# Ranks of a token tile in a PSUM bank of their own, and a new order of the steps behind the first half tiles

## The chip, the core and the metric

The kernel runs on one core of a Trainium2 chip. A core has a matrix engine (TensorE, in the rows PE, its weight loads PEld), VectorE (DVE), ScalarE (ACT), GpSimdE (POOL) and a queue that issues transfers (SyncE, SP); each runs its own list of instructions in the order in which the program was written, and semaphores hold an instruction until what it reads is there or what it overwrites has been read. Matrix products land in PSUM, in eight banks of 2 KB per partition. The metric is the time of one execution on the device in microseconds (us), as the median of several.

## The reference: what is computed

Three parts follow each other, on 4 x 768 = 3072 tokens with 8 heads of 48, so rows of 384:

```python
for t in range(S):                       # delta-rule attention, per batch and head
    y[:, :, t] = q_t @ state
    state = state + beta_t * outer(k_t, v_t - k_t @ state)
x = ((x @ w_a) * (x @ w_b)) @ w_out      # 384 -> 1536 -> 384
logits = x @ w_gate + modality_bias[modality_id]     # 8 experts
e = argmax(logits); gate = softmax(logits)[e]
out[token] = gate * (relu(x @ w1[e]) @ w2[e])        # 384 -> 1024 -> 384
```

All is float32; the kernel splits most operands into two float16 parts (hi and lo) and multiplies three of the four pairs.

## The kernel before

**Stages.** The attention is cut into 6 chunks of 128 steps by 4 batches, so 24 blocks `g` of 128 tokens. A block's steps have names by stage: `a_*` normalises the keys and makes their Gram matrix, `l_*` inverts a 32x32 triangle (a long chain of two VectorE operations per step, lines 621 and 626), `m1_mm` to `m4_mm` widen that inverse to 128, `p_*` makes the masked query-key product, and `s1_mm`, `s2_mm`, `s3_mm`, `s4_mm` carry the state. Two blocks make a token tile `t` of 256 rows for the second part: `f_mm(t, m)` is 18 matmuls for one of twelve 128-wide slices `m` of x @ w_a and x @ w_b (lines 334 to 336, PSUM tile `pab`); `f_a` copies one product (ACT, line 300, `a`), `f_ab` multiplies by the other (DVE, line 346), `f_hi` rounds to float16 (ACT, line 300, `g`), `f_lo` takes the rest (DVE or POOL, line 356, `g`), and `o_mm(t, m)` multiplies that slice by w_out and adds it into the two output tiles `po` (six matmuls, lines 367 to 369). The first token tile is worked as two half tiles, t = -2 and -1. `o_mm(t, 11)` completes a tile; then it is routed.

**Routing of a token tile.** `r_lg` (DVE, lines 388 to 394) makes logits, maximum, index and the one-hot tile `oh`; `r_mx` (lines 401 to 404) reduces both `po` tiles to their largest magnitude (`mo`); `r_hi` (ACT, line 410) and `r_lo` (DVE, line 416) read `po` again and write the rows. `r_rk` counts, with five matmuls of 8 columns on `oh` (lines 434 to 438), how many earlier tokens went to each expert, and `r_po` (DVE, lines 446 to 450) turns that into a slot number; `r_sc` scatters the row there. For the first ten tiles (`RQ = 10`) `r_rk` writes 24 columns behind the 392 columns of the tile's own `po` bank.

**The last part** gathers the rows per expert in slots `s` (`h_mm`, `g_mm`), with weights loaded and split on the way; it begins when the last token tile's products are done.

**What sets the order.** Every piece of work is a step declared with `do(...)`, which gives its engine, the steps it comes after and the buffers it takes. The table `ORDER` lists the 3613 steps by number; `emit` runs through it, and each engine executes its own steps in that sequence. `PICK` gives the engine of each step that could run on several. The PSUM pools bound what can be ahead: `ps_ab` has 2 banks for `pab`, `ps_o` two for `po`, `psg` two for the Gram, `m` and `p` steps, and `pss` two for the state steps (`pk`, `pu`, `py`, `pS`), all eight together. A step that takes a bank of a pool waits until the readers of the step that had it before are done.

Of the kernel before, what the change touches and what calls it, by code (L numbers as in the profile page):

```python
# [7 lines left out]
F32 = mybir.dt.float32  # L8
# [15 lines left out]
RQ = 10  # L24
# [167 lines left out]
def kernel(ctx, tc, k, q, v, beta, w_a, w_b, w_out, modality, w_gate, mbias, w1, w2, out):  # L192
    nc = tc.nc
    C, B, H, D = 6, 4, 8, 48
    NG = C * B
# [162 lines left out]
    def o_mm(t, m):  # L358
        g = GT[t, m]
        t, hs = (0, (t + 2,)) if t < 0 else (t, (0, 1))  # L360
        for h in hs:
            if m == 0:
                PO[2 * t + h] = ps_o.tile([128, WO + 3 * E], F32, name="po")
# [1276 lines left out]
```

## Time and profile before

| | |
|---|---|
| median of 3 runs | 959.95 us (955.12, 959.95, 961.57) |
| the profiled execution | 962.67 us, span 960.9 us |
| granted TensorE clock, mean | 0.949 |
| PE, PEld busy | 870.3 us (91%), 696.6 us (72%) |
| DVE, ACT, POOL busy | 722.1 us (75%), 542.6 us (56%), 299.9 us (31%) |

An engine's row of tenths shows its busy share in 40 slices of the span, PEclk the clock that was granted to TensorE in each. A row of waits says which engine's instruction sat idle for whose, the total, how often, and the longest. A matmul's row shows about 0.3 us for each, but the next one starts 0.11 to 0.17 us later, so that durations of neighbours overlap: what a group of matmuls costs is read from their starts.

### The profile page before, as it was taken

How to read it: one execution, taken by the hardware profiler on the slowest of the kernel's cores; microseconds unless marked ns; L12 is line 12 of the kernel's file. 1: busy time of each engine (PE TensorE's matmuls, PEld its weight loads, DVE VectorE, ACT ScalarE, POOL GpSimd, SP SyncE). 2: the span in 40 equal slices, each digit the busy share in tenths (PEclk: the TensorE clock that was granted, in tenths of full speed). 3: DMA queues.
4: the chain of work that ended last, by engine and by line, in shares of the span. 5: the costliest groups of instructions: out<-in, count | busy, mean ns of one | idle time of the engine just before them, and what ended most of it. 6: DMA issues, size and time to landing. Idle time of an engine off the chain costs nothing. (4 is left out here: it accounts for less than half of the span.)

```text
span 960.9 us, 30560 instructions
## 1 busy us (share of the span) xinstructions
PE 870.3 (91%) x11996; PEld 696.6 (72%) x11996; DVE 722.1 (75%) x1728; ACT 542.6 (56%) x1077; POOL 299.9 (31%) x442
## 2 busy tenths in 40 slices
PE   3446788799999999999999999999999999999996
PEld 1324577688777777888787888878878777878884
DVE  6899498776998799859995999454768885655551
ACT  3635676456754556656654655455466566555551
POOL 4421012433651344216331223023223342333331
PEclk9876659899999999999999999999999999999998
DMA  7896688684766546864667445432267899999980
GB/s 201 243 251 172 172 168 188 155 218 77 125 175 173 119 83 143 191 145 93 118 159 158 84 102 122 77 59 43 72 216 236 245 328 268 293 274 270 284 223 20
DMA packets 266066, 161.99 MB, mean 169 GB/s; under 512 B 188173, under 2 KB 245309, under 8 KB 265920
## 3 DMA queue, kind: packets, MB, share of 16 engines
q1 hardware_dynamic: 262288, 148.70, 64.0%
q0 software_dynamic: 3632, 11.29, 3.1%
q8 instruction: 99, 1.62, 0.7%
q14 instruction: 47, 0.39, 0.1%
HBM read 95.52 MB, written 30.31 MB: 131 GB/s over the span
## 5 line engine op out<-in xcount | busy, mean ns | idle before, releaser
L334 PE MATMUL pab<-xt,wa 128*128 128x256 f16 (+1 forms) x468 | 123.0, 267 | 1.9 <-DVE a L346 1.7
L335 PE MATMUL pab<-xt,wa 128*128 128x256 f16 (+1 forms) x468 | 122.7, 267 | 0.0
L336 PE MATMUL pab<-xt,wa 128*128 128x256 f16 (+1 forms) x468 | 122.7, 267 | 0.0
L334 PE MATMUL pab<-xt,wb 128*128 128x256 f16 (+1 forms) x468 | 122.4, 266 | 0.0
L335 PE MATMUL pab<-xt,wb 128*128 128x256 f16 (+1 forms) x468 | 122.4, 266 | 0.0
L336 PE MATMUL pab<-xt,wb 128*128 128x256 f16 (+1 forms) x468 | 122.4, 266 | 0.0
L303 DVE SCALAR_TENSOR_TENSOR w1l<-w1f,w1h 128x1024 f16<-128x1024 f32 x66 | 76.9, 1220 | 49.7 <-ACT w1h L300 39.4
L300 ACT ACTIVATE a<-pab 128x256 f32<-128x256 f32 (+1 forms) x156 | 56.6, 365 | 90.3 <-PE pab L336 66.9
L346 DVE SCALAR_TENSOR_TENSOR a<-pab,a 128x256 f32<-128x256 f32 (+1 forms) x156 | 61.9, 399 | 53.1 <-ACT a L300 52.0
L369 PE MATMUL po<-wo,g 128*128 128x392 f16 x288 | 95.8, 333 | 5.0 <-POOL g L356 2.4
L367 PE MATMUL po<-wo,g 128*128 128x392 f16 x288 | 95.7, 332 | 0.0
L368 PE MATMUL po<-wo,g 128*128 128x392 f16 x288 | 95.5, 332 | 0.0
L300 ACT ACTIVATE g<-a 128x256 f16<-128x256 f32 (+1 forms) x156 | 61.3, 397 | 45.5 <-DVE a L346 43.4
L1286 PE MATMUL pH<-xg_t,w1h 128*128 128x128 f16 x504 | 85.4, 219 | 0.0
L1287 PE MATMUL pH<-xg_t,w1h 128*128 128x128 f16 x504 | 85.4, 219 | 0.0
L1288 PE MATMUL pH<-xg_t,w1l 128*128 128x128 f16 x504 | 85.3, 219 | 0.0
L621 DVE TENSOR_TENSOR tmp<-A,T 128x31 f32<-128x31 f32 (+15 forms) x186 | 76.7, 412 | 2.1
L626 DVE TENSOR_TENSOR T<-T,tmp 128x31 f32<-128x31 f32 (+15 forms) x186 | 74.5, 400 | 2.0
L735 POOL TENSOR_TENSOR tl<-ttf,th 128x1024 f16<-128x1024 f32 x19 | 42.5, 2238 | 87.4 <-ACT th L300 57.8
L1315 PE MATMUL po<-w2h,hh 128*128 (+1 forms) x200 | 65.2, 326 | 2.1 <-ACT w1h L300 1.1
L300 ACT ACTIVATE w1h<-w1f 128x1024 f16<-128x1024 f32 x66 | 64.9, 1047 | 1.0 <-DMA w1f<-in_moe_w_dram 0.7
L1317 PE MATMUL po<-w2h,hl 128*128 (+1 forms) x200 | 65.2, 326 | 0.0
(315 smaller groups left out, 2825.1 us busy)
## 6 DMA issues: line engine op xcount, KB each, us to landing
w1f<-in_moe_w_dram SPq DMA_DIRECT2D x66, 512.0 KB
w2f<-in_moe_w_dram SPq DMA_DIRECT2D x32, 384.0 KB
gsc<-gs SPq DMA_DIRECT2D x22, 512.0 KB
bq<-aq SPq DMA_DIRECT2D x48, 128.0 KB
bk<-ak SPq DMA_DIRECT2D x40, 128.0 KB
qt<-in_q_dram SPq DMA_DIRECT2D x24, 192.0 KB
kt<-in_k_dram SPq DMA_DIRECT2D x24, 192.0 KB
raw<-in_moe_w_a_dram SPq DMA_DIRECT2D x12, 384.0 KB
```

The lines of the kernel that those rows point to most:

```text
L300: S_.activation(out=out, in_=in_, func=ACTF.Copy, scale=scale)
L303: V.scalar_tensor_tensor(out=out, in0=in_, scalar=scale, in1=hi, op0=ALU.mult, op1=ALU.subtract)
L334: T_.matmul(out=p[:, i], lhsT=wa[i][0][:, kk, sl], rhs=xt[:, kk], start=(kk == 0), stop=False)
L335: T_.matmul(out=p[:, i], lhsT=wa[i][0][:, kk, sl], rhs=xt[:, KD + kk], start=False, stop=False)
L336: T_.matmul(out=p[:, i], lhsT=wa[i][1][:, kk, sl], rhs=xt[:, kk], start=False, stop=(kk == KD - 1))
L367: T_.matmul(out=po, lhsT=g[:, 0, sl], rhs=wo[0][:, m], start=(m == 0), stop=False)
L368: T_.matmul(out=po, lhsT=g[:, 0, sl], rhs=wo[1][:, m], start=False, stop=False)
L369: T_.matmul(out=po, lhsT=g[:, 1, sl], rhs=wo[0][:, m], start=False, stop=(m == KF - 1))
L621: V.tensor_tensor(out=LN[c, 2], in0=A[:, j + 1 : 32, j : j + 1].to_broadcast([128, n, w]), in1=T[:, j : j + 1, 0:w].to_broadcast([128, n, ...
L1286: T_.matmul(out=pH[:, u], lhsT=wh[kk][:, sl], rhs=xt[:, kk], start=(kk == 0), stop=False)
L1287: T_.matmul(out=pH[:, u], lhsT=wh[kk][:, sl], rhs=xt[:, KD + kk], start=False, stop=False)
L1288: T_.matmul(out=pH[:, u], lhsT=wl[kk][:, sl], rhs=xt[:, kk], start=False, stop=(kk == KD - 1))
```

## The change

The rank counts get a tile of their own, `prk`, from the pool `pss` (its tag `ps`, which the state steps use too), for the first ten token tiles; `po` loses its 24 extra columns. So `po` no longer waits for `r_po` before it is given to the next token tile; `r_rk` takes one of the two `pss` banks until `r_po` has read it; `w_open`, which gives the attention's space to the last part, comes after `r_po(9)`. The numbers from the 1056th entry of `ORDER` on are new: of the steps, 302 of 669 on PE stand in another place in that engine's list (by 0.9 places in the mean over all, 7 at most), 643 of 1273 on DVE, 484 of 938 on ACT, 120 of 279 on POOL and 176 of 433 on SP. No step changes its engine, and none is added or removed.

```diff
-    2022, 1008, 1007, 989, 1982, 2026, 2023, 990, 1009, 2032, 2027, 947, 1010, 1985, 2028, 991, 2037, 2029, 992, 1031, 2033, 948, 1986, 1993, 993,
...
+    2441, 2442, 603, 1443, 1613, 2454, 2455, 1555, 1556, 2463, 1469, 646, 647, 648, 649, 2464, 2465, 2436, 2446, 1600, 2460, 2461, 1444, 2437, 2447,
...
@@ o_mm
-                PO[2 * t + h] = ps_o.tile([128, WO + 3 * E], F32, name="po")
+                PO[2 * t + h] = ps_o.tile([128, WO], F32, name="po")
@@ r_rk
-        pr = PO[2 * t][:, WO : WO + 3 * E] if t < RQ else M2["q"].tile([128, DM], F32, name="po2")[:, 0 : 3 * E]
-        R["pr"] = pr = pr.rearrange("p (i e) -> p i e", e=E)
+        if t < RQ:
+            R["pr"] = pr = pss.tile([128, 3, E], F32, name="prk", tag="ps")
+        else:
+            R["pr"] = pr = M2["q"].tile([128, DM], F32, name="po2")[:, 0 : 3 * E].rearrange("p (i e) -> p i e", e=E)
@@ the steps
-               take=[(f"ps_o{g % 2}", 1, [(r_hi, g), (r_lo, g), (r_lg, g // 2), (r_mx, g // 2), (r_po, g // 2)]) for g in ([t + 2] if half else [2 * t, 2 * t + 1])] if m == 0 else [])
+               take=[(f"ps_o{g % 2}", 1, [(r_hi, g), (r_lo, g), (r_lg, g // 2), (r_mx, g // 2)]) for g in ([t + 2] if half else [2 * t, 2 * t + 1])] if m == 0 else [])
-        do(r_rk, (t,), "PE", 0.1, o + 0.1, after=[(r_lg, t)] + ([(w_open,)] if t >= RQ else []), take=[("ps_q", 2, [(r_po, t)])] if t >= RQ else [])
+        do(r_rk, (t,), "PE", 0.27, o + 0.1, after=[(r_lg, t)] + ([(w_open,)] if t >= RQ else []), take=[("pss" if t < RQ else "ps_q", 2, [(r_po, t)])])
-    do(w_open, (), "-", 0.0, 0.0, after=[(c_end,)] + [(x_tr, g) for g in range(2, NG)] + [(p_lo, NG - 1, 1), (s3_lo, NG - 1), (l_o2, C - 1)])
+    do(w_open, (), "-", 0.0, 0.0, after=[(c_end,), (r_po, RQ - 1)] + [(x_tr, g) for g in range(2, NG)] + [(p_lo, NG - 1, 1), (s3_lo, NG - 1), (l_o2, C - 1)])
```

Lines behind 430 move down by two (the ranks' matmuls from 434 to 436, `r_po` from 446 to 448).

**The first place is on PE, the ranks of token tile 1.** The matmuls of `r_rk(1)` read the one-hot tile `oh` and write `po` before and `prk` now; `pab` is the up product of tile 2, `pk` is `s1_mm(8)`, `pg` the Gram step `a_mm(12)`. Before:

```order
L336 MATMUL pab_4403<-xt_3875,wb1_88 128x256
L434 LDWEIGHTS tri_92
L434 MATMUL po_3712<-oh_4394,tri_92 128x8
...
L438 MATMUL po_3712<-oh_4394,ones_93 128x8
L795 LDWEIGHTS ak_1634
L795 MATMUL pk_4450<-sst0_131,ak_1634 128x48
```

And now:

```order
L585 MATMUL pg_4507<-ak_4247,bk_4307 128x128
L436 LDWEIGHTS tri_92
L436 MATMUL prk_4531<-oh_4376,tri_92 128x8
...
L440 MATMUL prk_4531<-oh_4376,ones_93 128x8
L334 LDWEIGHTS wa0_85
L334 MATMUL pab_4555<-xt_3870,wa0_85 128x256
```

The ranks stood behind `f_mm(2,0)`; now `s3_mm(6)` and the two `a_mm` of block 12 stand between that and them, and two more `f_mm` and `s4_mm(6)` come before `s1_mm(8)`.

**The second place is on DVE, the same tile:** `lg` to `oh` is `r_lg`, `mo` and `io` are `r_mx`, and `pq` begins `r_po`, which frees the ranks' bank. Before:

```order
L394 TENSOR_TENSOR oh<-iota_95,ef 128x16
L401 TENSOR_REDUCE mo<-po 128x1 x2
...
L404 RECIPROCAL io<-mo 128x2
L303 SCALAR_TENSOR_TENSOR ul<-pu,uh 128x384
L346 SCALAR_TENSOR_TENSOR a<-pab,a 128x256
...
L416 SCALAR_TENSOR_TENSOR row<-po,io,row 128x384
...
L865 SCALAR_TENSOR_TENSOR xh<-py,iy,xh 128x384
...
L621 TENSOR_TENSOR tmp<-A,T 128x255
L446 TENSOR_TENSOR pq<-po,off 128x16
```

And now:

```order
L394 TENSOR_TENSOR oh<-iota_95,ef 128x16
L303 SCALAR_TENSOR_TENSOR ul<-pu,uh 128x384
L401 TENSOR_REDUCE mo<-po 128x1 x2
...
L404 RECIPROCAL io<-mo 128x2
L346 SCALAR_TENSOR_TENSOR a<-pab,a 128x256
L303 SCALAR_TENSOR_TENSOR wl<-w,wh 128x384
L319 TENSOR_REDUCE my<-py 128x1
...
L322 RECIPROCAL iy<-my 128x1
L448 TENSOR_TENSOR pq<-prk,off 128x16
```

`r_po(1)` stands behind five other steps where there were twenty.

**The third place is on PE, slices 5 to 10 of token tile 2.** Of each `f_mm` (`pab`) and `o_mm` (`po` with its slice `g`) one matmul is shown. Before:

```order
L334 MATMUL pab_5097<-xt_3875,wa0_85 128x256
...
L367 MATMUL po_4720<-wo0_89,g_4964 128x392
...
L367 MATMUL po_4720<-wo0_89,g_5093 128x392
...
L367 MATMUL po_4720<-wo0_89,g_5128 128x392
...
L367 MATMUL po_4720<-wo0_89,g_5154 128x392
...
L334 MATMUL pab_5182<-xt_3875,wa0_85 128x256
...
L334 MATMUL pab_5216<-xt_3875,wa0_85 128x256
```

And now:

```order
L334 MATMUL pab_5096<-xt_3870,wa0_85 128x256
...
L367 MATMUL po_4778<-wo0_89,g_4974 128x392
...
L367 MATMUL po_4778<-wo0_89,g_5074 128x392
...
L334 MATMUL pab_5149<-xt_3870,wa0_85 128x256
...
L334 MATMUL pab_5179<-xt_3870,wa0_85 128x256
...
L367 MATMUL po_4778<-wo0_89,g_5201 128x392
...
L367 MATMUL po_4778<-wo0_89,g_5207 128x392
```

Four `o_mm` stood in a row behind `f_mm(2,8)`, the last of them its own product; now `f_mm(2,9)` and `f_mm(2,10)` stand between the second and the third.

## Rows read from the trace of the kernel before

**Rows 1.** The page: span, TensorE's busy time, the granted clock in 40 slices.

```profile
span 960.9 us, 30560 instructions
PE 870.3 (91%) x11996; PEld 696.6 (72%) x11996; DVE 722.1 (75%) x1728; ACT 542.6 (56%) x1077; POOL 299.9 (31%) x442
...
PEclk9876659899999999999999999999999999999998
```

**Rows 2.** Busy time by stretch: PE, PEld, DVE, ACT, POOL, clock, DMA share, GB/s.

```profile
0.00:205.00 205.00, 136.36 (x1745) 103.32 (x1746) 165.89 (x406) 110.05 (x238) 60.65 (x108) 0.78 0.79 194
205.00:760.00 555.00, 543.53 (x8004) 442.35 (x8002) 438.56 (x1186) 325.22 (x697) 175.44 (x267) 1.00 0.57 132
...
240.00:600.00 360.00, 351.70 (x5445) 285.37 (x5443) 313.12 (x835) 215.39 (x460) 122.99 (x169) 1.00 0.61 132
```

**Rows 3.** Waits of PE and PEld, 200 to 770 us: total, times, longest.

```profile
PE po L434 <- DVE mo L401: 3.2, 4, 1.4
PE po L369 <- DVE g L356: 2.3, 5, 0.8
PE pab L334 <- DVE a L346: 1.7, 3, 0.8
PE py L848 <- DVE ul L303: 1.1, 2, 0.7
PE po L434 <- ACT row L410: 0.8, 1, 0.8
...
PEld L369 <- DVE g L356: 5.7, 9, 1.1
```

**Rows 4.** Order of time, the ranks of token tile 1.

```profile
269.35 0.17 DVE L394 TENSOR_TENSOR oh<-iota,ef 128x16 f16<-128x16 f32 x1
269.44 1.01 DVE L401 TENSOR_REDUCE mo<-po 128x1 f32<-128x384 f32 x2
...
270.05 0.17 PE L434 MATMUL po<-oh,tri 128*128 128x8 f16 x1 [1.35 <-DVE mo L401]
...
279.94 0.17 DVE L446 TENSOR_TENSOR pq<-po,off 128x16 f32<-128x16 f32 x1
...
280.62 0.17 DVE L450 CAST pi<-pf 128x2 int32<-128x2 f32 x1
```

**Rows 5.** Order of time, the ranks of token tile 3.

```profile
372.35 0.17 DVE L394 TENSOR_TENSOR oh<-iota,ef 128x16 f16<-128x16 f32 x1
...
373.04 0.17 PE L434 MATMUL po<-oh,tri 128*128 128x8 f16 x1 [0.65 <-DVE mo L401]
```

**Rows 6.** Order of time, the end of `o_mm(2, 8)` and the start of `f_mm(2, 9)`.

```profile
303.89 0.33 PE L368 MATMUL po<-wo,g 128*128 128x392 f16 x1
...
304.05 0.42 DVE L356 TENSOR_TENSOR g<-a,g 128x256 f16<-128x256 f32 x1
...
304.53 0.34 PE L369 MATMUL po<-wo,g 128*128 128x392 f16 x1 [0.31 <-DVE g L356]
...
304.70 0.33 PE L367 MATMUL po<-wo,g 128*128 128x392 f16 x1
...
305.20 0.27 PE L334 MATMUL pab<-xt,wa 128*128 128x256 f16 x1
...
305.31 0.27 PE L335 MATMUL pab<-xt,wa 128*128 128x256 f16 x1
```

**Rows 7.** Groups of instructions, 205 to 760 us: busy, mean ns, idle before.

```profile
L300 ACT ACTIVATE a<-pab 128x256 f32<-128x256 f32 (+1 forms) x134 | 50.6, 380 | 78.9 <-PE pab L336 61.5 <-DVE g L356 7.9 <-POOL g L356 5.8
L346 DVE SCALAR_TENSOR_TENSOR a<-pab,a 128x256 f32<-128x256 f32 (+1 forms) x134 | 55.6, 417 | 48.8 <-ACT a L300 48.2
L300 ACT ACTIVATE g<-a 128x256 f16<-128x256 f32 (+1 forms) x134 | 54.6, 412 | 41.6 <-DVE a L346 39.7 <-PE po L369 1.1 <-DVE sf L885 0.3
L356 DVE TENSOR_TENSOR g<-a,g 128x256 f16<-128x256 f32 x102 | 48.3, 478 | 14.8 <-ACT g L300 13.5 <-ACT ttf L300 1.0
```

**Rows 8.** Waits over the whole span, the costliest that a transfer ended.

```profile
PEld L765 <- DMA bq<-aq: 11.0, 2, 9.9
```

206 rows, old and new, of the table ORDER are left out of this document.

## The prediction, written before the result was known

> **What bounds the kernel now.** I read the page first. TensorE is busy for 91% of the span, and the clock that it was granted lies between 0.5 and 0.9 of full speed in the first eight slices of 24 us and in the top tenth from then on [rows 1]. Then the busy time by stretch: until 205 us TensorE works 136.36 of 205 us at a mean clock of 0.78; from 205 to 760 us it works 543.53 of 555 us at the full clock [rows 2]. On every engine the order is unchanged up to a place that lies between 225 and 231 us of this execution, and the slots behind 760 us keep nearly all of theirs. So what the new order can act on is the middle stretch, and there TensorE sets the pace: it sits idle for 555 - 543.53 = 11.5 us, 1.2% of the span. VectorE is close behind it, with 313.12 of 360 us between 240 and 600 us [rows 2], so a step that TensorE waits for is often not late in itself but stands in VectorE's line.
>
> Third, the waits say what those 11.5 us are [rows 3]: 3.2 + 0.8 = 4.0 us by the ranks' first matmul (five waits), 2.3 us by `o_mm` for the rest `g` that `f_lo` makes, 1.7 us by `f_mm` for a `pab` bank that `f_ab` still reads, and the other 3.5 us in small pieces, the largest 1.1 us by `s3_mm` for `ul`. The second is larger than it looks: the weight loads wait 5.7 us at nine places for the same `g`. A matmul of `o_mm` is shown for 0.33 us and the next starts 0.17 us later (304.53 and 304.70) [rows 6], so each such wait hides some 0.16 us under a row's end: 2.3 + 9 x 0.16 = 3.7 us.
>
> **The change, term by term.** Nothing is added: the five rank matmuls are the same five, with another target. All terms are of waits; a minus is a gain.
>
> *1. The ranks' wait.* In tile 1 `oh` is done at 269.35 + 0.17 = 269.52 us, but the first rank matmul starts at 270.05, right after the first of two reductions over `po` (269.44 + 0.55) [rows 4]. In tile 3 it is 372.52 and 373.04 [rows 5]. So 0.5 us of each wait are owed to a reader of the same `po` tile, and the rest is early arrival. With `prk` the first part goes. The second shrinks because ranks stand later: behind the tile's last `o_mm` there was TensorE work of 2.6, 2.4, 1.7, 2.3, 2.3 and 2.6 us in tiles 1, 2, 4, 5, 7 and 8, and now it is 4.5, 4.8, 5.2, 7.1, 5.8 and 3.9 us (steps between them in the two orders, at 18 x 0.11 = 2.0 us for an `f_mm` and 6 x 0.17 = 1.0 us for an `o_mm` by the starts in [rows 6], the others by their starts likewise). In tile 3 ranks keep their place and save 0.5 us. I take -3.6 of the 4.0 us. Bounds: -4.0 and 0.
>
> *2. `o_mm` waiting for `f_lo`.* From the end of `f_mm` four instructions follow one another, 0.38 + 0.42 + 0.41 + 0.48 = 1.7 us if no one is ahead of them [rows 7]. At the third place shown, `f_lo` ended at 304.47 and TensorE restarted at 304.53 [rows 6]. Of the 132 pairs of full tiles, 43 had less than 4.6 us of TensorE work between `f_mm` and its `o_mm`, and 12 have now; the median goes from 6.3 to 8.1 us. I scale the 3.7 us by 12/43 and get 1.0 left: -2.7. Bounds: -3.7, and 0 if VectorE's line is what is late.
>
> *3. `f_mm` waiting for its bank.* The price of those longer covers: places where three `f_mm` stand back to back, so that `f_a` and `f_ab` (0.80 us at least [rows 7]) have one `f_mm`'s 2.0 us, go from 5 to 14 of 130. The 1.7 us scaled by 14/5 would be 4.8, so +3.1 at most; only a chain that stands in line is late, so I take half: +1.5. Bounds: 0 and +3.1.
>
> *4. The state steps and the rest.* `s2_mm` to `s3_mm` has about the same covers (the shortest 1.8 us before, 1.4 now), `m1_mm` to `m2_mm` too (0.9 and 2.0). Of the 3.5 us I expect as much again: 0, between -3.5 and +3.5. The moved transfers (176 SP steps, by one place in the mean) cost TensorE almost nothing in this stretch; the nearest row of a late one is 11.0 us for two early in the span [rows 8], which keeps the upper end open.
>
> *5. The ranks' hold on a `pss` bank.* The second state step behind `r_rk` takes that bank, and so waits for `r_po`. In tile 1 ranks ran at 270.05 and `r_po` ended at 280.79, 10.7 us later [rows 4]; but that was with twenty VectorE steps between, and now there are five. The covers are 6.2, 6.3, 20.7, 7.0, 11.2, 10.4, 16.1, 14.3 and 3.2 us in tiles 0 to 8. With `r_po` close behind, only tile 8 is tight: +0.5. Bounds: 0, and what the second rival says.
>
> *6.* At nothing: `po` is free without `r_po`, since no row of waits has the first matmul of `o_mm` waiting for a bank; and `w_open` behind `r_po(9)`, since the loads that it opens also wait for the order of the experts, which needed `r_po(9)` already.
>
> **The sum:** -3.6 - 2.7 + 1.5 + 0 + 0.5 = -4.3 us. The profiled execution of 962.7 us would become 958.4; the median shown is 2.7 us below it, so 959.95 - 4.3 = **955.7 us**.
>
> **Rivals.**
>
> *The waits only change places (chance 0.26).* For it: with VectorE at 87% between 240 and 600 us [rows 2], a step moved forward there pushes another back, and 643 of its steps moved. Against it: 0.5 us per rank wait goes whatever VectorE does. Net -1 to +3 us, about 960.5 us.
>
> *The ranks hold up the state (0.10); this ends slower.* If VectorE reaches `r_po` as late as it did in tile 1, 10.7 us, the second state step waits 10.7 - cover where that is positive: 4.5 + 4.4 + 3.7 + 0.3 + 7.5 = 20.4 us over tiles 0, 1, 3, 5 and 8, of which -4.8 (the sum without term 5) takes back a part: 959.95 + 15.6 = 975.6 us. At 8 us it is 1.8 + 1.7 + 1.0 + 4.8 = 9.3, so 964.5. It decides from a hold of about 6 us; in tile 1's new order `r_po` has some 4 us of VectorE work ahead of it, which speaks against. The Trainium skill's page Perfetto Trace Analysis (Optimizing Tensor Performance, Matmuls) asks that independent matmul groups rotate through different PSUM banks, so that one is read while the next is written; by that rule a count of 24 columns that sits in one of two state banks stops the rotation, and the sum would be the 975.6 us of this rival. No run here shows it yet.
>
> *Nearly all waits go (0.14).* Terms 1, 2 and the small ones at their lower ends, -4.0 - 3.7 - 3.5, and term 3 at -1.7: -12.9, so 947 us. Against it: a line that is full at 87% will be late somewhere.
>
> *The change does not do what it says (under 0.02):* if ranks still waited for the reduction they would show that releaser; `prk` shares no bank with `po`, so I leave it inside the first rival.
>
> **How the numbers follow.** My forecast has the remaining 0.50, with a range of its own from -9 to -1 us (terms 1 and 2 at their ends, 3 and 4 halfway). The range of 8 in 10 reaches from 946 us (the third rival's better half left out) to 965 us (the second rival's milder end within). One per cent, 9.6 us, is about what a measurement of this kernel can tell from no change. Faster by more: the third rival and the edge of the forecast, 0.18. Slower by more: two thirds of the second rival, and a late transfer, 0.09. Within 1%: 0.73.
>
> **What would show it.** Step 1: no wait of the ranks' matmul for the `po` reduction, under 0.5 us in all. Step 2: the wait of `o_mm` for `g` at a third or less, in matmuls and in weight loads. Step 3: the wait of `f_mm` for `a` above 1.7 us. Step 5: no state step waiting for `r_po`. In all, TensorE idle for some 7 us between 205 and 760 us in place of 11.5, the time before 205 us and the last 200 us as they were. The prediction is wrong if the middle stretch's idle time is as it was or larger, or if the gain or loss lies outside that stretch.

## The result: slower by 0.9%

| | before | changed |
|---|---|---|
| median of 20 executions | 958.2 us (954.14 to 971.49) | 966.03 us (960.3 to 972.91) |
| ratio, 95% interval | | 1.0087 (1.0067 to 1.0106) |
| the profiled execution | 962.67 us, span 960.9 | 966.07 us, span 964.3 |

I had forecast 955.7 us and a range up to 965: the sign was wrong, and the time lies 1 us above the range. That the change stays within 1% had a chance of 0.73 in the prediction and came true, but by luck: the working behind it pointed the other way. With 20 executions of each, 0.9% can be told from no change.

The page of the changed kernel, for [rows 1]: span, busy time, granted clock in 40 slices of 24 us.

```profile
span 964.3 us, 30533 instructions
...
PE 872.7 (91%) x11996; PEld 699.9 (73%) x11996; DVE 732.2 (76%) x1728; ACT 542.0 (56%) x1077; POOL 279.5 (29%) x442
...
PEclk9967659899999999998999999999999999999999
```

An 8 stands in slice 19 (434 to 458 us), where [rows 1] has a 9. Busy time by stretch, for [rows 2], and below it three short ones; the third number from the end is the clock:

```profile
205.00:760.00 555.00, 539.78 (x7914) 439.57 (x7912) 442.73 (x1170) 320.74 (x691) 162.82 (x266) 0.99 0.58 129
...
430.00:434.40 4.40, 2.76 (x45) 1.71 (x44) 4.35 (x7) 1.06 (x3) 2.97 (x2) 0.98 0.48 92
434.40:437.60 3.20, 3.20 (x33) 2.03 (x32) 2.59 (x7) 0.92 (x3) 0.00 (x0) 0.50 0.20 61
437.60:450.80 13.20, 13.20 (x263) 11.55 (x262) 10.55 (x27) 10.30 (x22) 4.52 (x6) 1.00 0.37 73
```

TensorE is idle for 555 - 539.78 = 15.2 us of the middle stretch, where it was 11.5; by the prediction's own last sentence that makes it wrong. And after a wait of 1.6 us within 430 to 434.4 us its clock fell to 0.50, the 1.2 GHz level, for the 3.2 us shown (some 3.4 in all); it did so again at 454.7 us. The waits of TensorE from 200 to 770 us, for [rows 3]:

```profile
PEld L369 <- DVE g L356: 3.8, 6, 1.0
...
PE pab L334 <- DVE a L346: 2.7, 2, 2.1
...
PE py L853 <- DVE ul L303: 2.2, 3, 1.5
...
PE pe L672 <- DVE pm L772: 1.6, 1, 1.6
...
PE po L369 <- DVE g L356: 1.5, 3, 0.6
PE prk L436 <- DVE xh L867: 1.4, 2, 1.0
...
PE py L850 <- DVE ul L303: 0.9, 1, 0.9
PE pH L1288 <- DVE hl L1301: 0.8, 1, 0.8
...
PE prk L436 <- DVE oh L394: 0.4, 1, 0.4
```

The ranks' wait for the `po` reduction (`mo`) is gone, as intended. But `f_mm` now has one wait of 2.1 us for `a`, `m1_mm` (`pe`) waits 1.6 us for a Gram bank that `p_msk` reads, `s3_mm` waits 2.2 + 0.9 = 3.1 us for `ul` in place of 1.1, and the ranks wait 1.4 us for `xh`, the reader of the state's bank that they now share.

**Where the time went.** Both orders are the same up to about 225 us, and the start of `f_mm(1,6)` varies from 221.9 to 229.5 us over the profiled executions, with either order; of the 8.3 us between the two profiled executions of the kernel before, 5.7 lie ahead of it. So I compare from there on, by starts of first matmuls, with the idle time of 205 to 760 us beside (555 us less PE's busy time). The kernel before was timed again beside each group of runs: its median was 958.2 us beside the changed kernel, 959.8 beside x1 to x4, 959.11 beside y1 to y4 and 956.04 beside z1 to z3. So ratios are to be compared between groups, not medians.

| kernel (as labelled below) | f_mm(1,6) to h_mm(0,0), us | tiles 4 and 5 | tile 6 | h_mm(0,0) to end | idle | median | ratio to before |
|---|---|---|---|---|---|---|---|
| before | 523.3 | 106.5 | 43.5 | 209.9 | 11.5 | 958.2 | |
| before, second profile | 522.1 | 106.1 | 43.5 | 208.7 | 10.6 | | |
| changed | 530.0 | 112.3 | 45.5 | 211.3 | 15.2 | 966.03 | 1.0087 |
| changed, second profile | 525.5 | 107.4 | 45.5 | 211.4 | 13.7 | 964.66 | 1.0077 |
| x1_order_alone | 531.8 | 109.3 | 45.5 | 211.1 | 16.1 | 969.99 | 1.0128 |
| x2_bank_alone | 527.0 | 106.0 | 45.1 | 209.7 | 12.1 | 961.96 | 1.0021 |
| x3_tile5_old | 522.8 | 105.9 | 44.4 | 213.2 | 10.3 | 960.67 | 1.0016 |
| x4_triangle_back | 525.6 | 107.1 | 45.5 | 212.9 | 12.9 | 964.47 | 1.0068 |
| y1_after_quarters | 518.6 | 105.7 | 44.3 | 211.4 | 7.6 | 955.31 | 0.9973 |
| y2_before_quarters | 521.6 | 106.2 | 43.3 | 208.8 | 9.6 | 957.97 | 0.9992 |
| y3_tl_on_vector | 525.0 | 106.4 | 45.5 | 210.5 | 12.4 | 962.1 | 1.0040 |
| z1_tail_old | 526.8 | 109.3 | 45.5 | 210.2 | 12.7 | 962.77 | 1.0057 |
| z2_combined | 516.4 | 104.1 | 44.4 | 208.7 | 4.8 | 953.01 | 0.9944 |
| z3_eighths | 523.0 | 105.6 | 44.4 | 209.2 | 8.2 | 960.13 | 1.0019 |

(Tile 4 lasts from `f_mm(4,0)` to `f_mm(5,0)`, and so on; `o_mm(4,10)` and a state step moved across the border of tiles 4 and 5, so the two are read together.) In the first profile of the changed kernel tiles 4 and 5 lose 5.8 us and tile 6 2.0, the other tiles give 1.1 back, which makes the 6.7 us; the last part takes 1.4 us longer. In its second profile tiles 4 and 5 lose only 0.9 to 1.3 us, and tile 6 again 2.0.

**What happens in tile 5.** In order of time, the place of the first wait:

```profile
429.70 2.17 POOL L737 TENSOR_TENSOR tl<-ttf,th 128x1024 f16<-128x1024 f32 x1 [2.11 <-ACT th L300]
...
429.91 2.08 DVE L623 TENSOR_TENSOR tmp<-A,T 128x112 f32<-128x112 f32 x1
...
431.92 0.68 DVE L782 TENSOR_TENSOR pl<-pm,ph 128x512 f16<-128x512 f32 x1
...
432.52 0.41 DVE L346 SCALAR_TENSOR_TENSOR a<-pab,a 128x256 f32<-128x256 f32 x1
432.85 0.68 DVE L772 TENSOR_TENSOR pm<-pp,blm 128x512 f32<-128x512 f32 x1
...
433.58 0.24 PE L672 MATMUL pe<-tr,ge 32*32 32x32 f32 x2 [1.64 <-DVE pm L772]
...
449.13 2.26 POOL L737 TENSOR_TENSOR tl<-ttf,th 128x1024 f16<-128x1024 f32 x1
449.45 2.19 DVE L628 TENSOR_TENSOR T<-T,tmp 128x220 f32<-128x220 f32 x1
...
451.68 0.91 DVE L623 TENSOR_TENSOR tmp<-A,T 128x231 f32<-128x231 f32 x1
...
453.38 0.42 DVE L346 SCALAR_TENSOR_TENSOR a<-pab,a 128x256 f32<-128x256 f32 x1
...
453.85 0.27 PE L334 MATMUL pab<-xt,wa 128*128 128x256 f16 x1 [2.06 <-DVE a L346]
```

A triangle step, `l_mul(4,3)`, meets GpSimdE's subtraction `tl` (`m_lo`) and lasts 2.08 us; where it meets none, the same step takes 0.27 to 0.28 us. It ends 0.12 us behind `tl`. In VectorE's new list `pl`, `a` and `pm` stand behind it, and TensorE's `m1_mm(14)` behind `pm`. At 449.45 us it happens again with `l_sub(4,9)`; behind it come three more triangle steps, then the `a` for which `f_mm(5,8)` waits 2.06 us. In the order of before `f_ab(5,2)` and `p_msk(13,1)` stood ahead of `l_mul(4,3)`; `f_ab(5,6)` stood behind `l_sub(4,9)`, but ahead of the three triangle steps that follow it.

Not every VectorE instruction is held like this:

```profile
557.37 2.13 POOL L737 TENSOR_TENSOR tl<-ttf,th 128x1024 f16<-128x1024 f32 x1 [4.04 <-ACT th L300]
557.54 0.42 DVE L346 SCALAR_TENSOR_TENSOR a<-pab,a 128x256 f32<-128x256 f32 x1
558.28 0.42 DVE L346 SCALAR_TENSOR_TENSOR a<-pab,a 128x256 f32<-128x256 f32 x1 [0.31 <-ACT a L300]
...
480.21 2.13 POOL L737 TENSOR_TENSOR tl<-ttf,th 128x1024 f16<-128x1024 f32 x1 [4.69 <-DVE ix L392]
480.31 2.06 DVE L393 CAST ef<-ix 128x2 f32<-128x2 uint32 x1
```

`a`, with one operand in PSUM, takes its usual 0.42 us ([rows 7]) in the middle of a `tl`; a cast of two elements in SBUF takes 2.06 us in place of 0.17. The Trainium skill states the rule on its page SBUF — State Buffer, section Who interferes with whom: an instruction of VectorE with two SBUF inputs, or a cast or copy in a two-port mode, and an instruction of GpSimdE that reads SBUF lock each other out for the whole instruction. The trace agrees: 34 VectorE instructions began under one of the 18 `tl` between 220 and 760 us; the 16 with two SBUF operands or a cast ended 0.02 to 0.42 us behind it, and the 18 others (one operand in PSUM, a reduction, the maximum, the index search) kept their durations. I had not drawn on that page.

The changed kernel has no more of it than before: what VectorE's instructions between 220 and 760 us take beyond the tenth percentile of their own form, counted where it is over 0.15 us, adds up to 35.6 us in either (44 instructions before and 40 now). What differs is what stands behind them.

Two more places show it, and both are in either profile of the changed kernel:

```profile
260.44 2.03 DVE L303 SCALAR_TENSOR_TENSOR t1q<-qt,t1q 128x384 f16<-128x384 f32 x1
262.39 2.33 DVE L628 TENSOR_TENSOR T<-T,tmp 128x240 f32<-128x240 f32 x1
...
266.41 0.18 PE L853 MATMUL py<-ul,ph 128*128 128x48 f16 x1 [1.49 <-DVE ul L303]
...
487.25 0.17 PE L436 MATMUL prk<-oh,tri 128*128 128x8 f16 x1 [0.98 <-DVE xh L867]
```

At the first, two steps held by two `tl` one after the other stand ahead of `r_lg(1)` and `ul`, and `s3_mm(6)` waits 1.49 us for `ul`. In the order of before two triangle steps were held at the same place, ahead of the same `r_lg(1)`, and there the ranks waited, 1.35 us [rows 4]: the wait changed from one matmul to another. At the second, the cast of 2.06 us shown above is followed by VectorE work without a gap up to `xh`, for which the ranks of tile 5 wait at the start of tile 6.

### The profile page after: what moved, and what is told of

The parts are those of the page before. It is cut to its first block, busy times and chain, and to the rows that moved or that the text cites. A ratio compares the mean times of both kernels' runs of the same rounds, so it can differ in the third digit from the quotient of the medians.

```text
span 964.3 us, 30533 instructions
## 1 busy us (share of the span) xinstructions
PE 872.7 (91%) x11996; PEld 699.9 (73%) x11996; DVE 732.2 (76%) x1728; ACT 542.0 (56%) x1077; POOL 279.5 (29%) x442
## 5 line engine op out<-in xcount | busy, mean ns | idle before, releaser
L1318 PE MATMUL po<-w2l,hh 128*128 (+1 forms) x200 | 65.2, 326 | 0.0
```

## The experiments

**Order or bank?** `x1_order_alone` is the kernel before with the new table `ORDER` and nothing else.

> The kernel before with the new order of all steps alone: the ranks go on sharing the bank of their tile's po. Theory (the order carries the loss: in token tile 5 VectorE steps that TensorE waits for stand behind triangle steps that GpSimdE's subtraction tl stretches to 2 us, and the clock falls twice): the loss of 7.8 us stays, and up to 0.5 us for each of five rank waits on the po reduction comes back, so 965 to 968 us; tile 5, from the first f_mm of tile 5 to the first of tile 6, takes 66 to 69 us as in the changed kernel (67.1), not 59.4. Rival (the ranks' hold on one of the two pss banks holds up the state steps): without the hold the loss goes, 954 to 960 us, tile 5 at 58 to 61 us.

969.99 us, 1.0128 (1.0093 to 1.0162), above what was expected. The order alone carries the loss, and by the medians more of it, though the intervals overlap; the rival falls. Tile 5 takes 64.3 us, less than expected, with the wait at `f_mm(5,8)` and one stretch at half the clock. The new order needs the new bank: without it a single wait of the ranks, which was to be under 0.5 us, takes 2.6, and `pab` waits more often.

```profile
PE pab L334 <- DVE a L346: 5.5, 6, 2.2
PE po L434 <- DVE row L416: 2.6, 1, 2.6
```

`x2_bank_alone` is the changed code with the order of before:

```diff
 # moved against the order of before
+r_po(1) ahead of s1_mm(8)
+r_rk(5) behind s1_w(16), r_rk(7) behind s1_w(20), r_po(5) and r_po(7) after them
+w_open behind r_po(9)
```

> The changed kernel's code (ranks in a pss bank) with the order of before. Only what the bank forces is moved: r_po(1) goes ahead of s1_mm(8), r_rk(5) and r_rk(7) a place or two back. Theory (the order carries the loss): 957 to 960 us, tile 5 at 59 to 61 us; the waits of the ranks' matmul for the po reduction (4.0 us before) shrink by 0.5 us each. Rival (the ranks' hold on a pss bank carries it): 964 to 970 us, with waits of pk, pu or py matmuls for r_po's readers in the list of waits.

961.96 us, 1.0021 (0.9998 to 1.0045): at most 0.45% slower; the median is 2 us above what was expected. Tile 5 takes 58.7 us, a little less than expected. But the bank is not free in that order, for its holds show:

```profile
PE pk L797 <- DVE off L449: 1.5, 1, 1.5
PE prk L436 <- DVE oh L394: 1.5, 3, 0.9
...
PE pS L882 <- DVE off L449: 0.5, 1, 0.5
```

The ranks' wait goes from 4.0 us to 1.5, and 2.0 us come back as waits of state steps for `r_po` (`off`). So the mechanism of the second rival exists, at 2 us where the rival had 20.

**Tile 5 alone.** `x3_tile5_old` takes the stretch between two `f_mm` from the old order:

```diff
 # changed kernel's ORDER up to f_mm(5,0)
-the next steps up to f_mm(6,0) as in the new order
+the next steps up to f_mm(6,0) as in the order of before
 # the rest in the new order
```

> The changed kernel, where only the steps between the first f_mm of token tile 5 and the first of tile 6 stand in the order of before (85 VectorE and 43 TensorE steps in another place); all other steps keep the new order. Theory (the loss sits in tile 5): tile 5 goes from 67.1 to 59 to 61 us, the clock does not fall between 410 and 480 us, and the whole takes 957 to 960 us. Rival (the loss is spread over the new order, and one profiled execution showed it in tile 5 by chance): 963 to 967 us, with the lost time in other tiles.

960.67 us, 1.0016 (0.9989 to 1.0044), a little above what was expected. Tile 5 takes 59.1 us, the clock stays at 1.00, and the loss is gone from the middle stretch, where the idle time is 10.3 us. It is a matter of this one stretch, or of what it does to the next (tile 6 gains 1.1 us too). The edit moves steps on all engines there, so by itself it doesn't say which of them matter.

**Which steps of it?** `x4_triangle_back` moves triangle steps on VectorE:

```diff
+p_lo(13,0), f_ab(5,2), p_msk(13,1),
 l_mul(4,0), l_sub(4,0), ..., l_mul(4,3),
-p_lo(13,0), f_ab(5,2), p_msk(13,1),
...
+f_ab(5,6),
 l_mul(4,9), l_sub(4,9), ..., l_mul(4,11),
-f_ab(5,6),
```

> The changed kernel with two edits of VectorE's list in token tile 5: the triangle steps l_mul(4,0) to l_mul(4,3) go behind p_lo(13,0), f_ab(5,2) and p_msk(13,1), and l_mul(4,9) to l_mul(4,11) behind f_ab(5,6). TensorE's list is untouched. Theory (a triangle step stretched to 2 us by GpSimdE's tl, ahead of what TensorE waits for): TensorE's two waits of 1.8 and 2.2 us at m1_mm(14) and f_mm(5,8) go, and with them the two stretches of 3.4 us at half the clock (1.7 us each); tile 5 takes 60 to 63 us and the whole 959 to 962 us. The stretched instructions themselves stay, at other places. Rival (VectorE is simply late by its load in tile 5): waits of the same size reappear within tile 5, which stays above 65 us, the whole at 964 to 967 us.

964.47 us, 1.0068 (1.0040 to 1.0096), not told from the changed kernel. The two waits did go, and no low clock shows, but the waits from 410 to 490 us are now led by these:

```profile
PEld L369 <- DVE g L356: 2.6, 3, 1.3
PE po L369 <- DVE g L356: 1.5, 2, 0.9
```

The triangle steps that were put back are held all the same (`l_sub(4,9)` for 2.20 us), and what now stands behind them, `f_lo`'s `g`, is late instead. Tile 5 takes 62.1 us, as expected, but that is what the second profile of the changed kernel has too (62.4). The expectation was too simple: the wait changed places.

**Chance?** `y4_after_again` is the changed kernel once more.

> The changed kernel itself, once more, for a second profiled execution and a time on the same chip as its variants. Theory: token tile 5 takes 64 to 68 us again, with TensorE's wait at f_mm(5,8) and at least one stretch at half the clock, since order and durations are the same in each execution; 964 to 968 us. Rival (tile 5 was slow by chance in the one profiled execution): tile 5 below 62 us, with the loss elsewhere.

964.66 us, 1.0077 (1.0052 to 1.0103). Of tile 5's two waits only the one at `f_mm(5,8)` is there (2.17 us), tile 5 takes 62.4 us, below what I had expected, and the clock does not fall: `tl` began 1.0 us after `l_mul(4,3)`, where in the first profile it began 0.2 us before it, and so it held `f_lo(5,2)` instead (1.73 us). So the first wait belongs to that execution. The second wait belongs to the order: it is in all four profiles that have this list of steps on VectorE in tile 5 (2.06 us in the changed kernel, 2.17 here, 2.18 in x1, 2.17 in z1), and behind it the granted clock fell to 0.50 for some 3.4 us in three of them, not in this one. The second profile of before (one execution, 954.42 us):

> The kernel before itself, for a second profiled execution. Theory: from the seventh slice of token tile 1 to the last part (f_mm(1,6) to h_mm(0,0)) it takes 522 to 525 us again, tile 5 59 to 60 us, the last part 209 to 210 us, and no stretch at half the clock; what differs is the time ahead of f_mm(1,6) (222.3 to 229.5 us so far, in both orders). Rival (tile 5 jumps in this order too): tile 5 above 62 us.

It agrees (tile 5: 59.2 us; the last part, 208.7 us, is a little shorter than expected), so the loss of the middle stretch is 2.2 to 7.9 us between these pairs of profiles.

**The stretch taken away.** `y3_tl_on_vector` leaves the triangle steps where they are:

```diff
-    "m_lo": "VPVVVVPPPPPPPPPPPPPPPPPP",
+    "m_lo": "VPVVVVPPPPPPVVPPPPPPPPPP",
 # and m_lo(12) behind f_lo(5,2), m_lo(13) behind s4_g(12)
```

> The changed kernel with the subtractions tl of blocks 12 and 13, the two that fall into token tile 5's waits, on VectorE (1.22 us each by the five that already run there), behind f_lo(5,2) and s4_g(12). The triangle steps keep their places ahead of p_lo(13,0), f_ab(5,2), p_msk(13,1) and f_ab(5,6). Theory (the stretch decides): l_mul(4,3) and l_sub(4,9) take 0.3 us each, TensorE's waits at m1_mm(14) and f_mm(5,8) fall below 0.7 us, the clock does not fall, tile 5 takes 61 to 64 us, the whole 960 to 963 us. Rival (the places of the triangle steps alone make VectorE late): both waits stay above 1.2 us and tile 5 above 65 us, the whole 965 to 968 us.

962.1 us, 1.0040 (1.0018 to 1.0061), 2.6 us below the changed kernel timed beside it, whose interval (1.0052 to 1.0103) overlaps. The row of the step and of what followed it:

```profile
431.48 0.28 DVE L623 TENSOR_TENSOR tmp<-A,T 128x112 f32<-128x112 f32 x1
...
450.82 0.42 DVE L346 SCALAR_TENSOR_TENSOR a<-pab,a 128x256 f32<-128x256 f32 x1
...
451.30 0.27 PE L334 MATMUL pab<-xt,wa 128*128 128x256 f16 x1 [0.38 <-DVE a L346]
```

With the same triangle steps ahead, the wait of 2.17 us is 0.38. So that wait is made by the hold, not by the places alone. It is one wait, and the gain is small: from `f_mm(1,6)` to `h_mm(0,0)` the profile shows 525.0 us against 525.5, and 1.0 us less in tiles 4 and 5.

**Shorter holds, everywhere.** `y1_after_quarters` and `y2_before_quarters` are the two kernels with one line changed:

```diff
-        eng_of(m_lo, g).tensor_tensor(out=tl, in0=tt, in1=TH[g], op=ALU.subtract)
+        for h in range(0, H, 2): eng_of(m_lo, g).tensor_tensor(out=tl[:, h : h + 2], in0=tt[:, h : h + 2], in1=TH[g][:, h : h + 2], op=ALU.subtract)
```

> The changed kernel with GpSimdE's subtraction tl (128x1024, 2.13 us, 19 of them on GpSimdE) issued as four instructions of 128x256; nothing else moves. Theory (a VectorE instruction of two SBUF operands waits for the whole GpSimdE instruction that it meets, so it is the length of one instruction that makes a triangle step of 0.3 us last 2.1): no triangle step is above about 1 us under tl any more, the two waits of TensorE in token tile 5 (1.8 and 2.2 us) shrink below 1 us each, the clock does not fall there, tile 5 takes 61 to 64 us in place of 67, and the whole 959 to 962 us. Rival (the two engines share a bandwidth, so that the overlap costs VectorE the same in pieces): the sum of the stretches stays at some 35 us and the whole within 2 us of the changed kernel's 966.

> The kernel before with the same edit: tl in four instructions of 128x256 on each engine that has it. Theory: its VectorE stretches fall too (35.7 us between 220 and 760 us), but few of them stand ahead of what TensorE waits for, so the gain is smaller than in the changed kernel: 0 to -3 us, 957 to 960 us. Rival (TensorE's idle time follows the sum of the stretches, wherever they stand): as large a gain as in the changed kernel, 4 to 6 us, 954 to 956 us.

955.31 us, 0.9973 (0.9943 to 1.0002), and 957.97, 0.9992 (0.9965 to 1.0018). The new order gains 9.3 us against the changed kernel timed beside it (intervals apart) and is no longer the slower one; the old order gains 1.1 us, which can't be told from nothing. In the changed kernel's tile 5 a triangle step now waits for a quarter:

```profile
444.67 3.15 POOL L737 TENSOR_TENSOR tl<-ttf,th 128x256 f16<-128x256 f32 x4
444.98 0.74 DVE L628 TENSOR_TENSOR T<-T,tmp 128x220 f32<-128x220 f32 x1
445.76 0.75 DVE L623 TENSOR_TENSOR tmp<-A,T 128x231 f32<-128x231 f32 x1
446.54 0.75 DVE L628 TENSOR_TENSOR T<-T,tmp 128x231 f32<-128x231 f32 x1
...
448.47 0.27 PE L334 MATMUL pab<-xt,wa 128*128 128x256 f16 x1 [1.26 <-DVE a L346]
```

Where a step of 2.19 us, one of 0.91 and two of 0.4 stood (3.9 us in all), there are now four of some 0.75 (3.0 us), and `f_mm(5,8)` still waits 1.26 us, more than the 1 us that I had expected. The gain of the whole is larger than expected because it is not tile 5's alone: of the 6.9 us against the second profile of the changed kernel only 1.7 lie in tiles 4 and 5; the two places shown above take part in it, for the waits for `ul` fall from 3.1 to 1.1 us and no wait of the ranks is left in the list. The rival's sum of holds fell too, from 36 to 26.7 us, in the old order from 35.6 to 28.2 with next to no gain; so the sum alone is not what counts.

**The last part, and all together.**

> The changed kernel with the steps behind the first f_mm of token tile 11 in the order of before. Theory (a second, smaller part of the loss sits at the start of the last part: h_mm(1,0) waits 0.8 us for hl, because r_ex(11) on ScalarE and r_se(11) on VectorE now stand ahead of h_hi(0,0) and h_lo(0,0), and slot 7 takes 12.8 us in place of 11.9): the time from h_mm(0,0) to the end goes from 211.3 to about 209.7 us, the wait of pH for hl is gone, and the whole is 1 to 2 us below the changed kernel, 963 to 965 us. Rival (the tail's 1.5 us come from arrivals of weights by transfer, not from these places): the tail stays at 211 us or more.

962.77 us, 1.0057 (1.0030 to 1.0083), by the time alone not told from the changed kernel; the last part took 210.2 us. In the changed kernel `r_se(11)` stands ahead of `h_lo(0,0)`:

```profile
757.14 0.17 DVE L459 RECIPROCAL se<-se 128x2 f32<-128x2 f32 x1
...
757.32 0.69 DVE L1301 SCALAR_TENSOR_TENSOR hl<-pH,hh 128x512 f16<-128x512 f32 x1
...
758.07 0.23 PE L1288 MATMUL pH<-xt,w1e 128*128 128x128 f16 x1 [0.75 <-DVE hl L1301]
```

With the old places no matmul of `pH` waits, and slot 7 takes 11.9 us in place of 12.8 to 13.0. One profile is little, but the table has fourteen: the last part takes 208.7 to 210.2 us in the seven with the old places behind `f_mm(11,0)`, and 210.5 to 213.2 in the seven with the new ones.

`z2_combined` joins four edits:

```diff
+the quarters of tl
+f_ab(5,6) ahead of l_mul(4,9)
+r_rk(5) behind f_mm(6,2)
+the steps behind f_mm(11,0) in the order of before
```

> The changed kernel with four edits together: tl in four instructions; l_mul(4,9) to l_mul(4,11) behind f_ab(5,6); r_rk(5) behind f_mm(6,2), so that it does not wait for the state's pss bank; and the steps behind the first f_mm of tile 11 in the order of before. Theory (the losses add up): 955.3 us of the quarters alone, less 1.4 us at f_mm(5,8), 0.7 us at r_rk(5) and 1.5 us in the tail, so 951 to 953 us, 6 to 8 us below the kernel before. Rival (each wait that goes comes back at the next late step): 954 to 957 us, as with the quarters alone.

953.01 us, 0.9944 (0.9912 to 0.9975): the fastest of all here, 0.6% below before. The time is at the upper end of what was expected, but that is partly luck: it is 3.0 us below the kernel before timed beside it, where I had expected 6 to 8, and its interval overlaps with that of the quarters alone (0.9943 to 1.0002). What the three further edits add is seen in the profile (4.9 us less from `f_mm(1,6)` to the end than in `y1_after_quarters`) and not shown by the times. The middle stretch:

```profile
205.00:760.00 555.00, 550.20 (x8047) 448.93 (x8045) 445.87 (x1205) 328.91 (x701) 179.62 (x322) 1.00 0.59 135
```

TensorE is idle for 4.8 us. The order that lost 0.9% is not slower than the one of before once the holds are short.

> The same as the combined kernel, but tl in eight instructions of 128x128. Theory: the longest stretch of a VectorE instruction under tl falls to some 0.4 us, but by the step from 2.13 us for one instruction to 4 x 0.67 a further 0.14 us per instruction is paid, so that tl takes some 3.3 us and the state's second product waits for it a little more often: within 2 us of the combined kernel, 950 to 955 us. Rival (only the sum of the stretches counts): it falls again, and 2 to 4 us with it.

960.13 us, 1.0019 (0.9995 to 1.0043): 7.1 us above the combined kernel with quarters, so the expectation failed. The sum of the holds is the least of all, some 18 us, but `tl` itself is late:

```profile
PE pu L828 <- POOL tl L737: 2.7, 10, 0.3
```

Eight instructions of 0.43 us make 3.4 us where one took 2.13, so that the state's second product (`s2_mm`) waits for `tl` ten times. TensorE's idle time grows by 3.4 us (8.2 against 4.8). The rest is in waits too short to show as idle time, since rows of matmuls overlap: from the first to the last start of their 24 matmuls, the 20 `s2_mm` of the middle stretch take 19.3 us together in place of 13.7, which is 5.6 of the 6.6 us by which that stretch grows.

## Why the prediction was wrong

**The step that failed is term 4**, the state steps and the rest at nothing, and under it an assumption that I did not state: that VectorE's instructions keep their durations when they are put in another order. My covers were counted in TensorE work against chains of [rows 7]; ten VectorE instructions that are held for over 1 us between 220 and 760 us stood in the trace of before, and I read none of them (the new order has thirteen). The waits that I left at 3.5 us grew by 4.4: `ul` from 1.1 to 3.1, the Gram bank by 1.6, `pH` by 0.8; my bound had been +3.5. In the second profile it is 2.8, without the Gram bank. Terms 1 and 2 were too large besides, by 1.4 and 1.5 us.

- **Term 1**, the ranks' wait: -3.6 was forecast, 4.0 became 0.4 + 1.4 = 1.8, so -2.2. The `po` reduction is gone from the list; in tile 1, for [rows 4], nothing is waited for:

```profile
265.71 0.17 DVE L394 TENSOR_TENSOR oh<-iota,ef 128x16 f16<-128x16 f32 x1
...
268.23 0.17 PE L436 MATMUL prk<-oh,tri 128*128 128x8 f16 x1
```

  What came instead is the state's bank: ranks wait until `s3_lo` has read it. I had priced the hold in one direction only. And the largest of the waits that went, 1.35 us in tile 1, had two held triangle steps ahead of it; the holds stayed, and `s3_mm(6)` now waits 1.49 us there.
- **Term 2**, `o_mm` for `g`: -2.7 was forecast; by the same count 3.7 became 1.5 + 6 x 0.16 = 2.5, so -1.2. That longer covers help less where VectorE is held is argued, not shown.
- **Term 3**, `f_mm` for `a`: +1.5 was forecast, 1.7 became 2.7. The size is near, the cause is another: one wait of 2.1 us behind a held triangle step, not three `f_mm` in a row.
- **Term 5**, the hold by the ranks: no wait for `r_po` in the changed kernel. `x2_bank_alone` shows it in the old order, 2.0 us. The rule of the Trainium skill that I had weighed (Perfetto Trace Analysis, Optimizing Tensor Performance, Matmuls: rotate through banks) points the right way: state steps wait 2.0 us for `r_po` in the old order, and in the new one it is the ranks that wait, 1.4 us for the bank. Both are far from the rival's 20 us; it fell.
- **Term 6** stood, but "the last 200 us as they were" did not: 208.7 to 209.9 us became 211.3 and 211.4, with the new places of the steps behind `f_mm(11,0)` (z1 and the fourteen profiles).
- The clock at half for twice 3.4 us, some 1.7 us of loss each, was in no term. In the second profile it does not fall; in x1 and z1 it falls once in tile 5.

Added up for the first profile, -2.2 - 1.2 + 1.0 + 4.4 = +2.0 us and 3.4 by the clock make 5.4 of the 8.1 us that are lost behind `f_mm(1,6)` (6.7 + 1.4); the other 2.7 are in small waits that I have not put down one by one. In the prediction's overview of [rows 1] one reading is off: the last slice of the clock is in the ninth tenth, not in the top one, which changes nothing here.

The first rival, that waits only change places, came nearest in kind: its -1 to +3 us for the middle stretch against +2.2 to +7.9.

What is shown: the order, not the bank, carries the loss (x1, x2); the long holds of VectorE instructions by one GpSimdE instruction are what makes this order slower than the old one (y1, with y2 as the counterpart; y3 for one wait); undoing one stretch of it (x3) or shortening the holds (y1) is enough. Only argued: why this order suffers more. It lists triangle steps in longer runs (2.7 in a row in the mean where there were 1.5, over the part that is new), with the steps that TensorE waits for behind the run; but `x4_triangle_back`, which broke up two of these runs, gained nothing that can be told.

## What to carry to other kernels

Before an order is changed, look in the trace for instructions of one line whose longest duration is several times their median, and ask what they overlap with: such an instruction has a price that belongs to its neighbours on another engine, and it moves with the order. Where an engine's long instruction locks out another, try it in pieces, and count what the pieces cost: four gained 9.3 us here, and eight in place of four lost 7.1 in the combined kernel, because the cut instruction itself came late. A price of a shared bank has two directions, who waits for the newcomer and whom the newcomer waits for.

## What the runs showed that I had not expected

- A cast of 128x2 elements can last 2.06 us on VectorE (usually 0.17) beside a GpSimdE subtraction; the maximum and the index search of the same routing step keep their 0.16 us there.
- GpSimdE is held as well: in `y3_tl_on_vector` its `t1k` (0.92 us in the median) took 2.82 us beside VectorE's `tl`, and 1.70 us at the same place in `y1_after_quarters`, without that `tl`.
- Waits of TensorE of 1.6 and 2.1 us were each followed by some 3.4 us at the 1.2 GHz level in one profile. The wait of 2.2 us at the second of these places was followed by such a stretch in x1 and z1 too, but not in the second profile of the changed kernel.
- GpSimdE's subtraction costs 2.13 us for 1024 elements per partition, 4 x 0.67 = 2.7 in quarters, 8 x 0.43 = 3.4 in eighths.
